# Attention and two feed-forward layers on one core: ScalarE's table load moved behind the last pair's copy, and a planner with other step times and due times

## The chip, the core and the metric

The program runs on one NeuronCore of a Trainium2 chip. TensorE (PE in the rows) multiplies, VectorE (DVE), ScalarE (ACT) and GpSimd (POOL) work on tiles, and SyncE (SP) issues the transfers. The metric is the device time of one execution in microseconds; lower is better.

## The reference

```python
# q, k, v: (4, 12, 448, 64); weights 768 x 2048 and 2048 x 768, twice
q_n, k_n = rmsnorm(q, g_q), rmsnorm(k, g_k)
scores = q_n @ k_n^T / sqrt(64); attn = softmax(scores)
x = (attn @ v) transposed to 1792 tokens x 768
h = x @ w_in;   x = (h * sigmoid(h)) @ w_out      # layer 1
h = x @ w2_in;  out = (max(h, 0) ** 2) @ w2_out   # layer 2
```

## The kernel before

**Stages.** Attention takes 24 pairs of heads one after the other, to about 271 us. Layer 1 takes the tokens in two halves (two batches of 448 tokens each) and the 2048 inner columns in four quarters, which makes eight segments, up to about 737 us. Layer 2 again takes two halves, and in each eight groups of 256 inner columns. Every product is made in higher precision from two parts of each operand: an upper part (a cast), a lower part (a subtraction), and three products. In most of layer 1 and all of layer 2 the products of 2 x 2 blocks are made by seven instead of eight block products (function `seven`, line 1104, nine matmuls of 448 columns each); only the first segment multiplies plainly (`up`, line 1017). The down products stand on line 1201 (layer 1, 448 columns), and on lines 1443 and 1568 (layer 2, 384 columns).

**Weights.** They arrive as 64-bit numbers. `words` loads a block into `raw` (two buffers, line 913, on SyncE's queue), and ScalarE makes the upper word (`magnitude`, line 920) and the lower bits (`low`, line 925); VectorE joins them (`merge`, line 932). `parts` splits the result into an upper and a lower part (lines 549 or 551, and 558).

**Order.** A hand-written table gives the times of all attention steps and fixes their order. All other steps are ordered by a planner (class `Plan`) when the program is built: it goes through the steps with a duration for each engine on which a step may run, and takes at each point the step that can start first, by its due time among equals. So it also chooses between VectorE, ScalarE and GpSimd for copies, casts and subtractions. Its inputs are the durations (`dve_t`, `pool_t`, `any_t`, `pe_t`, `SWITCH`, `PROD`) and `DUE`, a table that moves the due times of kinds of steps by stage. Each engine then runs its own list in that order, and waits where data or a buffer is missing.

**ScalarE's table.** `exp` in attention and `silu` in layer 1 need different tables of the engine. The program has no call for the load; it stands in ScalarE's list right ahead of the first activation that needs it: before, the first `silu`.

**The place after attention.** TensorE makes the first products of layer 1 into three PSUM banks of tag `t`, and a bank comes free when `silu` (line 1029) has read it. The last pair's result is copied out of PSUM by ScalarE (`pv_copy`, line 537).

Of the kernel before, what the change touches and what calls it, by code (L numbers as in the profile page):

```python
# [8 lines left out]
F32 = mybir.dt.float32  # L9
# [3 lines left out]
AF = mybir.ActivationFunctionType  # L13
# [3 lines left out]
P = 128  # L17
# [81 lines left out]
class Step:  # L99
# [10 lines left out]
LAG = {"pe": 0.21, "act": 0.13, "dve": 0.12, "pool": 0.12, "sp": 1.9, "none": 0.0}  # L110
SELF = {"pe": 0.0, "act": 0.1, "dve": 0.1, "pool": 0.06, "sp": 1.9, "none": 0.0}
FORM = {"scores": "rows", "attend": "columns"}
SWITCH = 0.16
ENGINES = ("pe", "act", "dve", "pool", "sp", "none")
ROUNDS = 8
AHEAD = 25.0
DUE = {
    "end0": {"acc": 4.25, "down2": -1, "h_hi": 21.25, "h_lo": 3.75, "keep_parts2": -1.25, "load_y": -0.75, "p1_copy": 3.75, "prod": 0.25, "square": 1, "u_sum": -0.5, "w_hi2": -6, "w_lo2": -0.75, "w_sum": -0.75, "y_hi": 5.25, "y_lo": 4.25, "y_sum": -3.5},
    "end1": {"acc": 2, "down2": -11.25, "h_hi": 16, "h_lo": 2.5, "h_sum": -39.5, "join": 18, "keep_parts2": -11.75, "load_parts2": -2.25, "load_word2": 1.75, "load_y": 0.5, "p1_copy": 0.5, "prod": 2, "square": 21.25, "store": -1.25, "u_sum": -1, "w_hi2": 4.25, "w_sum": -4.5, "y_lo": -3, "y_sum": 2.5},
    "now": {"ident": 5.75, "swap_pools": -0.5},  # L120
    "seg0": {"add": -0.5, "down": 3, "g_hi": 0.5, "g_lo": 0.75, "keep": 10.25, "load_raw": -6, "load_y": 0.5, "low": 1, "magnitude": -2, "merge": -6, "out1": -1, "p1_copy": 4, "part": 0.5, "prod": 4.75, "silu": 0.5, "store_y": -1, "u_sum": 2.75, "up": 2.5, "w_hi": 4.5, "w_lo": 6.25, "w_sum": -2, "y_hi": 0.75, "y_lo": 1, "y_sum": 2},
    "seg1": {"add": -4.25, "down": -4.5, "g_hi": 2.25, "g_lo": 5, "keep2": 45.25, "load_raw2": 6, "load_word": -5.5, "load_y": -0.75, "low2": -1.5, "magnitude2": -3, "merge2": -4.5, "p1_copy": -6.25, "part": -3.75, "prod": -3.25, "silu": -5.75, "store_y": 7, "u_sum": 2.25, "w_hi": 1.75, "w_lo": 1, "w_sum": -3, "y_hi": 10, "y_lo": 0.75, "y_sum": 2.5},
}


# [280 lines left out]
def kernel(  # L406
# [13 lines left out]
    nc = tc.nc  # L420
# [51 lines left out]
    def dve_t(n, rate=960.0, lock=False):  # L472
        return {"dve": (0.07 + n / rate, None, lock)}

    def pool_t(n, rate=474.0):
        return {"pool": (0.145 + n / rate, None, True)}

    def any_t(n, rate=474.0):
        return {**dve_t(n, 960.0, True), **pool_t(n, rate)}

    def copy_t(n):
# [2 lines left out]
    def pe_t(t):  # L484
        return {"pe": (t, None, False)}
# [13 lines left out]
    for n, src in enumerate((g_q, g_k)):  # L499
        for h in range(2):  # L500
# [4 lines left out]
                writes=[(graw, (n, h))],  # L505
# [46 lines left out]

        step(kind, when, copy_t(n), copy, reads=reads, writes=writes)

    def lower_part(kind, when, o, a, h, n, reads, writes, rate=474.0):

        step(
            kind, when, any_t(n, rate), lambda e: engine(e).tensor_tensor(o(), a(), h(), ALU.subtract),  # L558
            reads=reads, writes=writes,
        )  # L560

    def prepare(i):
# [88 lines left out]
        for n in range(2):  # L651
            n32 = sa([CP, NCH, 2, D], F32, "n")
            step(
                "norm", at, any_t(W2, 600.0),
                lambda e, n=n, n32=n32: engine(e).tensor_tensor(
                    n32.ap.rearrange("p c h d -> p h c d"),
                    qk.ap[:, n].rearrange("p (h c) d -> p h c d", h=2),
                    y.ap[:, n].rearrange("p (h c) -> p h c", h=2).unsqueeze(3).to_broadcast([CP, 2, NCH, D]),
                    ALU.mult),
                reads=[y, (qk, n)], writes=[n32],  # L660
            )
            plan.fix(i, "norm", j=n, at="dve" if i < 2 else "pool")
            pt = psum("t")

            def turn(e, n32=n32, pt=pt):
                for c in range(NCH):
                    nc.tensor.transpose(  # L667
                        pt.ap[:, c * CP:(c + 1) * CP], n32.ap[:, c].rearrange("p h d -> p (h d)"), ident.ap)

            step("turn_q", at, pe_t(0.384), turn, reads=[n32, ident], writes=[pt])  # L670
            plan.fix(i, "turn_q", j=n)

            def upper(e, n=n, pt=pt):
                o, a_ = T.ap[:, n, 0], pt.ap[:, :S]
# [32 lines left out]
    def weigh(i, T):  # L707

        PT = [sa([CP, NB8, CT, CP], F32, "PT") for _ in range(NCH // CT)]
        sums = sb([CP, 2, NCH], F32, "sum", 3)  # L710
        for c in range(NCH):
            at = ("pair", i, c)
            E = sa([CP, 2, S], F32, "E")
            pts = [psum("s"), psum("s")]

            def scores(e, c=c, pts=pts):
                for k_, (a, b_) in enumerate(((0, 0), (0, 1), (1, 0))):
                    for j in range(2):
                        r = slice(j * D, (j + 1) * D)
                        nc.tensor.matmul(  # L720
                            pts[j].ap[:CP, :S], T.ap[r, 0, a, c * CP:(c + 1) * CP], T.ap[r, 1, b_],
                            start=(k_ == 0), stop=(k_ == 2),
                        )

            step("scores", at, pe_t(0.606), scores, reads=[(T, (n, a)) for n in range(2) for a in range(2)], writes=pts)
            plan.fix(i, "scores", c)
            for j, pt in enumerate(pts):
                mx = sa([CP, 1], F32, "mx", 6)
                step(
                    "row_max", at, {"dve": (0.535, None, False)},  # L730
                    lambda e, pt=pt, mx=mx: nc.vector.tensor_reduce(  # L731
                        mx.ap, pt.ap[:CP, :S], AX.X, ALU.max, negate=True),
                    reads=[pt], writes=[mx],
                )
                plan.fix(i, "row_max", c, j)
                step(
                    "exp", at, {"act": (0.62, None, False)},
                    lambda e, j=j, c=c, pt=pt, mx=mx, E=E: nc.scalar.activation(  # L738
                        E.ap[:, j], pt.ap[:CP, :S], AF.Exp, bias=mx.ap, accum_out=sums.ap[:, j, c:c + 1]),
                    reads=[pt, mx], writes=[(E, j), (sums, (j, c))],  # L740
                )
                plan.fix(i, "exp", c, j)
                pe = psum("t")

                def turn(e, j=j, pe=pe, E=E):
                    for m in range(NCH):
                        nc.tensor.transpose(  # L747
                            pe.ap[:CP, m * CP:(m + 1) * CP], E.ap[:, j, m * CP:(m + 1) * CP], ident.ap)

                step("turn_e", at, pe_t(0.384), turn, reads=[(E, j), ident], writes=[pe])  # L750
                plan.fix(i, "turn_e", c, j)
                copy_step(
                    "e_copy", at, ECOPY[c][j], lambda c=c, j=j: PT[c // CT].ap[:, j * NCH:(j + 1) * NCH, c % CT, :],
                    lambda pe=pe: pe.ap[:CP, :S].rearrange("p (m t) -> p m t", t=CP), S, [pe], [(PT[c // CT], (c % CT, j))],
                )
                plan.fix(i, "e_copy", c, j)
        return PT, sums

    def attend(i, vr, PT, sums):
# [32 lines left out]
        for c2, pt in enumerate(PT):  # L792

            def products(e, c2=c2, pt=pt):
# [9 lines left out]
                        )  # L804

            step(
                "attend", at, pe_t(1.456), products,
                reads=[vr] + [(pt, (c, j)) for c in range(CT) for j in range(2)], writes=[(pv, c2)],
            )
            plan.fix(i, "attend", c2)  # L810
# [4 lines left out]
            "pv_copy", at, ("act", "dve"), lambda: t.ap, lambda: pv.ap[:, :S], S,  # L815
            [(pv, c2) for c2 in range(len(PT))], [t])
        plan.fix(i, "pv_copy", at="act")
        step(
            "attended", at, any_t(S),
            lambda e: engine(e).tensor_tensor(t.ap, t.ap, R.ap, ALU.mult),  # L820
# [216 lines left out]
    FD = 2  # L1037
    halves = {}
    W3 = HC * P
    PROD = 9 * 0.2065  # L1040

    def view(b, a, c):

# [641 lines left out]
```

## Time and profile before

| | us |
|---|---|
| median of 3 runs | 1165.32 |
| lowest and highest | 1164.49, 1168.14 |
| the profiled execution | 1167.08 |
| its span, first to last instruction | 1165.3 |
| TensorE busy in it | 1147.8 |
| VectorE, ScalarE, GpSimd busy | 939.3, 632.3, 287.9 |

In the rows a line such as `PE t L1104` names the engine, the tile that is written and the line of the program. A duration of a matmul holds its pipeline, so consecutive ones overlap; how fast they follow each other is read from their starts. The granted clock (PEclk) is the share of 2.4 GHz that TensorE was given: 1.00 is 2.4 GHz, 0.50 is 1.2 GHz.

### The profile page before, as it was taken

The numbers are of one execution on the slowest core, as the hardware profiler recorded it, in microseconds if no ns is written. First come the engines' busy times: TensorE is split into PE (matmuls) and PEld (weight loads), VectorE is DVE, ScalarE is ACT, GpSimd is POOL, SyncE is SP. The second block draws the span as 40 slices with busy tenths as digits, with TensorE's granted clock in tenths as the row PEclk, the third lists the DMA queues.
The fourth block names the chain that finished last, engine by engine and source line by source line (L and its number), as shares of the span: only waits on it lengthen the run. The fifth ranks groups of instructions, "written<-read, shape, count | busy, mean of one in ns | idle before, by whom it ended". The sixth has DMA issues, their size and how long they took to land.

```text
span 1165.3 us, 19244 instructions
## 1 busy us (share of the span) xinstructions
PE 1147.8 (99%) x6817; PEld 1018.8 (87%) x6817; DVE 939.3 (81%) x1685; ACT 632.3 (54%) x1290; POOL 287.9 (25%) x507
## 2 busy tenths in 40 slices
PE   7999999998999999999999999999999999999998
PEld 5777777777999999999999999999998999999997
DVE  7888888886876868996878698588888976888876
ACT  5999999985554444555535353543433535333321
POOL 4566676632000101210111021001121120122220
PEclk8999999999999999999999999999999999999999
DMA  6566768578855564778776849977777696555444
GB/s 175 94 103 115 105 109 111 99 125 175 275 167 185 172 212 133 263 236 273 244 238 209 272 145 329 337 271 261 286 264 260 217 378 230 177 176 190 164 163 135
DMA packets 142064, 235.22 MB, mean 202 GB/s; under 512 B 32016, under 2 KB 105744, under 8 KB 141968
## 3 DMA queue, kind: packets, MB, share of 16 engines
q1 hardware_dynamic: 141728, 233.80, 67.2%
q8 instruction: 54, 0.88, 0.3%
q14 instruction: 42, 0.34, 0.1%
q10 hardware_dynamic: 240, 0.20, 0.1%
HBM read 157.58 MB, written 76.37 MB: 201 GB/s over the span
## 4 chain that ended last, share of the span: by engine, by line
PE 91%; DVE 4%; ACT 2%; DMA 1%; issue 1%; SPq 0%; POOL 0%; ACTq 0%; DVEq 0%; POOLq 0%
PE t L1104 22%; PE s L1201 20%; PE s L1443 11%; PE pv L1104 9%; PE t L747 7%; PE pv L797 7%; PE s L720 6%; PE s L1568 6%; PE t L1017 2%; PE t L667 2%; DMA raw<-in_moe_w_out_dram 1%; DVE gg L1462 1%; DVE w L558 1%; DVE g L1119 0%; DVE g L1500 0%
## 5 line engine op out<-in xcount | busy, mean ns | idle before, releaser
L1201 PE MATMUL s<-gg,w 128*128 128x448 f32 x1152 | 240.4, 367 | 0.0
L1201 PEld LDWEIGHTS s<-gg,w 128*128 128x128 f32 x1152 | 216.2, 188 | 19.8 <-DVE g L1213 0.3
L1119 DVE TENSOR_TENSOR g<-t,g 128x448 f32<-128x448 f32 x180 | 108.8, 619 | 63.9 <-PE t L1104 53.1
L1443 PE MATMUL s<-w,gh 128*128 128x384 f32 (+1 forms) x564 | 143.0, 334 | 2.1 <-DVE gg L1462 1.1
L738 ACT ACTIVATE E<-s,mx 112x448 f32<-112x448 f32 x192 | 122.9, 653 | 13.7 <-ACT xf L537 7.9
L731 DVE TENSOR_REDUCE mx<-s 112x1 f32<-112x448 f32 x192 | 107.4, 611 | 14.4 <-PE s L720 14.1
L1462 DVE TENSOR_TENSOR gg<-s,gg 128x384 f32<-128x384 f32 (+1 forms) x197 | 102.6, 547 | 18.1 <-PE s L1443 17.7
L558 DVE TENSOR_TENSOR w<-W,w 128x768 fp32r<-128x768 f32 (+1 forms) x123 | 111.7, 917 | 4.2 <-ACT w L549 3.3
L1443 PEld LDWEIGHTS s<-w,gh 128*128 128x128 f32 x564 | 101.8, 188 | 4.0 <-DVE gg L1462 1.9
L1104 PE MATMUL t<-yb,w 128*128 128x448 f32 x468 | 103.1, 367 | 0.2 <-DVE w L558 0.2
L747 PEld LDWEIGHTS t<-ident,E 112*112 112x112 f32 x768 | 73.8, 134 | 32.5 <-issue 19.1
L549 ACT CAST w<-W 128x768 fp32r<-128x768 f32 (+1 forms) x74 | 54.9, 744 | 83.8 <-PE s L1201 31.9
L747 PE MATMUL t<-ident,E 112*112 112x112 f32 x768 | 94.7, 266 | 1.2 <-ACT E L738 1.2
L1368 ACT ACTIVATE g<-g 128x448 f32<-128x448 f32 x48 | 27.7, 578 | 124.6 <-DVE g L1119 124.1
L1443 PE MATMUL s<-w,gl 128*128 128x384 f32 (+1 forms) x282 | 94.3, 335 | 0.3 <-POOL gl L558 0.3
L1104 PEld LDWEIGHTS t<-yb,w 128*128 128x128 f32 x468 | 87.6, 188 | 8.1 <-DVE w L558 0.5
L797 PE MATMUL pv<-PT,vv 112*64 112x224 f32 x768 | 83.0, 359 | 0.1
L720 PE MATMUL s<-T 64*112 64x448 f32 x576 | 73.8, 388 | 1.3 <-ACT T L676 1.2
L1104 PE MATMUL pv<-xb,w 128*128 128x448 f32 x324 | 72.4, 367 | 0.0
L539 DVE COPY PT<-t 112x448 f32<-112x448 f32 x96 | 59.1, 618 | 11.6 <-PE t L747 11.5
L797 PEld LDWEIGHTS pv<-PT,vv 112*64 112x64 f32 x768 | 51.0, 136 | 20.0 <-ACT xf L537 0.3
L1104 PEld LDWEIGHTS pv<-xb,w 128*128 128x128 f32 x324 | 60.7, 188 | 5.5
(168 smaller groups left out, 2213.1 us busy)
## 6 DMA issues: line engine op xcount, KB each, us to landing
raw<-in_moe_w_in_dram SPq DMA_DIRECT2D x32, 768.0 KB
raw<-in_moe_w_out_dram SPq DMA_DIRECT2D x24, 512.0 KB
raw<-in_moe_w_out_dram SPq DMA_DIRECT2D x16, 768.0 KB
su<-w SPq DMA_DIRECT2D x16, 768.0 KB
w<-su SPq DMA_DIRECT2D x16, 768.0 KB
xf<-y SPq DMA_DIRECT2D x48, 224.0 KB
xf<-x SPq DMA_DIRECT2D x39, 224.0 KB
ki<-W SPq DMA_DIRECT2D x16, 384.0 KB
```

The source lines that it names most:

```text
L558: kind, when, any_t(n, rate), lambda e: engine(e).tensor_tensor(o(), a(), h(), ALU.subtract),
L720: nc.tensor.matmul(pts[j].ap[:CP, :S], T.ap[r, 0, a, c * CP:(c + 1) * CP], T.ap[r, 1, b_], start=(k_ == 0), stop=(k_ == 2),)
L731: lambda e, pt=pt, mx=mx: nc.vector.tensor_reduce(mx.ap, pt.ap[:CP, :S], AX.X, ALU.max, negate=True),
L738: lambda e, j=j, c=c, pt=pt, mx=mx, E=E: nc.scalar.activation(E.ap[:, j], pt.ap[:CP, :S], AF.Exp, bias=mx.ap, accum_out=sums.ap[:, j, c:c ...
L747: nc.tensor.transpose(pe.ap[:CP, m * CP:(m + 1) * CP], E.ap[:, j, m * CP:(m + 1) * CP], ident.ap)
L797: nc.tensor.matmul(pv.ap[j * D:(j + 1) * D, c2 * CT * CP:(c2 + 1) * CT * CP], vr.ap[:, j * NCH + m, :], pt.ap[:, j * NCH + m].rearrange("p ...
L1104: nc.tensor.matmul(pt.ap[:, :S], w_()[:, c0 + c, :], view(b, a, c)(), start=(start and c == 0 and k == 0), stop=(c == HC - 1 and k == 2), ...
L1119: lambda e: nc.vector.tensor_tensor(o.ap, pt.ap[:, :S], a.ap, ALU.add),
L1201: nc.tensor.matmul(pt.ap[:, :S], w_()[:, f, :], gg.ap[:, k, a, f, :], start=(f == 0 and n == 0), stop=(f == HQ - 1 and n == 2),)
L1443: nc.tensor.matmul(pt.ap[:, :en], g.ap[:, fi, c0:c0 + P], w_()[:, 0, e0:e0 + en], start=(n == 0), stop=(n == 5),)
L1462: "acc", at, dve_t(n), lambda e: nc.vector.tensor_tensor(o(), pt.ap[:, :n], o(), ALU.add),
L1568: nc.tensor.matmul(pt.ap[:, :NH], a[i][0](m), b[j][0](), start=(start and k == 0), stop=(k == 2), skip_group_check=True,)
```

## The change

Three things change. First, a new step `table` behind the last pair's `pv_copy`: a `silu` of one column, whose result nobody reads, so that the table load stands there. Second, durations in the planner: GpSimd's subtraction of 448 columns goes from 1.09 to 1.18 us, transposes from 0.384 to 0.406, `attend` from 1.456 to 1.512, `PROD` from 1.8585 to 1.8252, `SWITCH` from 0.16 to 0.13. Third, other numbers in `DUE`. The arithmetic that the output is made of stays the same.

```diff
-SWITCH = 0.16
+SWITCH = 0.13
...
 DUE = {
...
-    "now": {"ident": 5.75, "swap_pools": -0.5},
+    "now": {"ident": 12.75},
...
-    def pool_t(n, rate=474.0):
-        return {"pool": (0.145 + n / rate, None, True)}
+    def pool_t(n, rate=415.0):
+        return {"pool": (0.1 + n / rate, None, True)}
...
-            step("turn_q", at, pe_t(0.384), turn, reads=[n32, ident], writes=[pt])
+            step("turn_q", at, pe_t(0.406), turn, reads=[n32, ident], writes=[pt])
...
-                "attend", at, pe_t(1.456), products,
+                "attend", at, pe_t(1.512), products,
...
         plan.fix(i, "pv_copy", at="act")
+        if i == len(pairs) - 1:
+            first = sb([P, 1], F32, "first", 1)
+            step(
+                "table", ("seg", 0, 0.0), {"act": (1.4, None, False)},
+                lambda e: nc.scalar.activation(first.ap, t.ap[:, :1], AF.Silu), reads=[t], writes=[first],
+            )
...
-    PROD = 9 * 0.2065
+    PROD = 9 * 0.2028
```

The new lines move later line numbers by 6 (line 1029 becomes 1035). The order of every engine is the same up to the end of attention, except for three places of `magnitude` and `low` in ScalarE's list. What follows are places where it differs.

ScalarE's list from the last pair's copy (`xf<-pv`) on; `W<-raw` and `raw<-raw` are `magnitude` and `low`, `g<-t` is `silu`. Before:

```order
L537 COPY xf<-pv 128x448
L920 ACTIVATE W<-raw 128x512
L925 ACTIVATE raw<-raw 128x512
L1029 ACT_TABLE_LOAD
L1029 ACTIVATE g<-t 128x448
L549 CAST gg<-g 128x448
```

And with the change:

```order
L537 COPY xf<-pv 128x448
L822 ACT_TABLE_LOAD
L822 ACTIVATE first<-xf 128x1
L549 CAST w<-W 128x768
L926 ACTIVATE W<-raw 128x512
L931 ACTIVATE raw<-raw 128x512
L1035 ACTIVATE g<-t 128x448 x2
L549 CAST gg<-g 128x448
```

The load moved ahead of `magnitude`, a cast of 768 columns came from VectorE's list, and the first two `silu` stand together.

VectorE's list at the third to last group of layer 2's first half, up to the accumulation (`gg<-s,gg`) for which TensorE waits at 881.01 us of the trace; `g<-t,g` adds products, `W<-W` are `w_sum`, `gl`, `v` and `w` from two operands are lower parts. Before:

```order
L1119 TENSOR_TENSOR g<-t,g 128x448 x2
L1462 TENSOR_TENSOR gg<-s,gg 128x384
L1119 TENSOR_TENSOR g<-t,g 128x448
L1062 TENSOR_TENSOR W<-W 128x384
L551 CAST v<-W 128x384
L1062 TENSOR_TENSOR W<-W 128x384
L558 TENSOR_TENSOR gl<-g,gh 128x448
L1081 TENSOR_TENSOR W<-W 128x384
L1462 TENSOR_TENSOR gg<-s,gg 128x384
```

And with the change:

```order
L1125 TENSOR_TENSOR g<-t,g 128x448
L558 TENSOR_TENSOR gl<-g,gh 128x448
L1125 TENSOR_TENSOR g<-t,g 128x448 x2
L1068 TENSOR_TENSOR W<-W 128x384 x2
L558 TENSOR_TENSOR v<-W,v 128x384
L1087 TENSOR_TENSOR W<-W 128x384
L551 CAST gh<-g 128x448
L1468 TENSOR_TENSOR gg<-s,gg 128x384
```

Two lower parts `gl` and the lower part of `v` came from GpSimd, the cast of `v` went to ScalarE, and an accumulation went ahead of the piece. Further ahead a square of `g` and a cast of 768 columns went to ScalarE.

TensorE's list at the end of layer 2's first half, ahead of the first down product of the last group (`s<-w,gh`, with `s<-w,gl` behind it). Before:

```order
L1104 MATMUL pv<-xb,w 128x448 x9
L1104 MATMUL t<-xc,w 128x448 x9
L1104 MATMUL t<-part,w 128x448 x9
L1443 MATMUL s<-w,gh 128x384 x2
L1443 MATMUL s<-w,gl 128x384
```

And with the change:

```order
L1110 MATMUL t<-xc,w 128x448 x9
L1110 MATMUL t<-part,w 128x448 x9
L1110 MATMUL pv<-raw,w 128x448 x9
L1449 MATMUL s<-w,gh 128x384 x2
L1449 MATMUL s<-w,gl 128x384
```

A product of the second half, nine matmuls, came ahead of the down product. Over the whole program GpSimd's list has 19 instructions less, VectorE's 6 more and ScalarE's 14 more.

## Rows read from the trace of the kernel before

**Rows 1.** The page's first part: busy time, share of the span, instructions.

```profile
PE 1147.8 (99%) x6817; PEld 1018.8 (87%) x6817; DVE 939.3 (81%) x1685; ACT 632.3 (54%) x1290; POOL 287.9 (25%) x507
```

**Rows 2.** TensorE's waits after 300 us: total us, times, longest.

```profile
PE s L1568 <- DVE part L558: 1.1, 2, 0.8
PE s L1443 <- DVE gg L1462: 1.1, 1, 1.1
PE s L1443 <- DVE gh L551: 0.8, 1, 0.8
PE s L1443 <- POOL gl L558: 0.3, 1, 0.3
PE t L1104 <- DVE w L558: 0.2, 1, 0.2
```

**Rows 3.** The chain that ended last, at the first `w_out` block: start, us.

```profile
269.79 10.34 DMA raw<-in_moe_w_out_dram
```

**Rows 4.** Timeline of ScalarE: start, us, instruction [idle before <- releaser].

```profile
271.70 0.53 ACT L537 COPY xf<-pv 128x448 f32<-128x448 f32 x1 [1.30 <-PE pv L797]
280.20 0.66 ACT L920 ACTIVATE W<-raw 128x512 f32<-128x512 f32 x1 [7.97 <-DMA raw<-in_moe_w_out_dram]
...
281.42 1.28 ACT L1029 ACT_TABLE_LOAD   x1
282.71 0.54 ACT L1029 ACTIVATE g<-t 128x448 f32<-128x448 f32 x1
```

**Rows 5.** Timeline of TensorE behind its wait in the first segment.

```profile
283.31 2.58 PE L1017 MATMUL t<-xc,w 128*128 128x448 f32 x9 [3.00 <-ACT g L1029]
285.69 6.83 PE L1017 MATMUL t<-xb,w 128*128 128x448 f32 x27
292.36 0.99 PE L1017 MATMUL t<-xc,w 128*128 128x448 f32 x4
```

**Rows 6.** Stretches: length, busy us (instructions) by engine, PEclk, DMA share, GB/s.

```profile
284.00:288.00 4.00, 4.00 (x14) 3.55 (x14) 4.00 (x7) 2.19 (x4) 1.22 (x1) 0.59 1.06 335
288.00:292.00 4.00, 4.00 (x21) 3.65 (x20) 3.20 (x7) 2.24 (x4) 1.56 (x1) 0.99 0.54 191
300.00:511.00 211.00, 211.00 (x1022) 191.63 (x1021) 173.05 (x297) 103.97 (x174) 19.04 (x13) 1.00 0.63 201
515.00:735.00 220.00, 220.00 (x1087) 203.59 (x1086) 170.73 (x284) 107.37 (x170) 30.74 (x22) 1.00 0.75 250
```

**Rows 7.** Timeline of TensorE where the second token half begins.

```profile
511.85 2.10 PE L1104 MATMUL t<-xc,w 128*128 128x448 f32 x9
513.79 2.03 PE L1104 MATMUL t<-xb,w 128*128 128x448 f32 x9
515.65 1.98 PE L1104 MATMUL t<-yb,w 128*128 128x448 f32 x9
517.47 0.57 PE L1104 MATMUL pv<-gh,w 128*128 128x448 f32 x2
```

**Rows 8.** Timeline of all engines at the accumulation wait in layer 2.

```profile
878.24 1.83 POOL L558 TENSOR_TENSOR w<-W,w 128x768 fp32r<-128x768 f32 x1 [0.35 <-ACT w L549]
878.29 2.20 DVE L1081 TENSOR_TENSOR W<-W 128x384 f32<-128x384 f32 x1
...
880.88 0.54 DVE L1081 TENSOR_TENSOR W<-W 128x384 f32<-128x384 f32 x1
...
881.01 0.61 PE L1443 MATMUL s<-w,gh 128*128 128x384 f32 x2 [1.13 <-DVE gg L1462]
...
881.34 0.61 DVE L558 TENSOR_TENSOR gl<-g,gh 128x448 fp32r<-128x448 f32 x1
```

**Rows 9.** Stretches, columns as in rows 6: end of the first half; layer 2.

```profile
450.00:512.00 62.00, 62.00 (x301) 56.10 (x301) 56.53 (x100) 32.02 (x56) 12.22 (x8) 1.00 0.61 204
737.00:1166.00 429.00, 420.65 (x2222) 397.17 (x2220) 343.05 (x615) 163.29 (x298) 74.85 (x62) 1.00 0.64 230
```

**Rows 10.** Timeline of TensorE at a wait for weights in layer 2.

```profile
773.05 1.89 PE L1104 MATMUL t<-yb,w 128*128 128x448 f32 x8 [0.19 <-DVE w L558]
```

More of the change, by code (lines that the diff above doesn't have):

```diff
@@ L117 @@
 DUE = {
-    "end0": {"acc": 4.25, "down2": -1, "h_hi": 21.25, "h_lo": 3.75, "keep_parts2": -1.25, "load_y": -0.75, "p1_copy": 3.75, "prod": 0.25, "square": 1, "u_sum": -0.5, "w_hi2": -6, "w_lo2": -0.75, "w_sum": -0.75, "y_hi": 5.25, "y_lo": 4.25, "y_sum": -3.5},
-    "end1": {"acc": 2, "down2": -11.25, "h_hi": 16, "h_lo": 2.5, "h_sum": -39.5, "join": 18, "keep_parts2": -11.75, "load_parts2": -2.25, "load_word2": 1.75, "load_y": 0.5, "p1_copy": 0.5, "prod": 2, "square": 21.25, "store": -1.25, "u_sum": -1, "w_hi2": 4.25, "w_sum": -4.5, "y_lo": -3, "y_sum": 2.5},
@@ L120 @@
-    "now": {"ident": 5.75, "swap_pools": -0.5},
-    "seg0": {"add": -0.5, "down": 3, "g_hi": 0.5, "g_lo": 0.75, "keep": 10.25, "load_raw": -6, "load_y": 0.5, "low": 1, "magnitude": -2, "merge": -6, "out1": -1, "p1_copy": 4, "part": 0.5, "prod": 4.75, "silu": 0.5, "store_y": -1, "u_sum": 2.75, "up": 2.5, "w_hi": 4.5, "w_lo": 6.25, "w_sum": -2, "y_hi": 0.75, "y_lo": 1, "y_sum": 2},
-    "seg1": {"add": -4.25, "down": -4.5, "g_hi": 2.25, "g_lo": 5, "keep2": 45.25, "load_raw2": 6, "load_word": -5.5, "load_y": -0.75, "low2": -1.5, "magnitude2": -3, "merge2": -4.5, "p1_copy": -6.25, "part": -3.75, "prod": -3.25, "silu": -5.75, "store_y": 7, "u_sum": 2.25, "w_hi": 1.75, "w_lo": 1, "w_sum": -3, "y_hi": 10, "y_lo": 0.75, "y_sum": 2.5},
+    "end0": {"down2": -1.5, "h_hi": 50.5, "h_lo": -0.75, "keep_parts2": 4.25, "load_y": -0.25, "prod": -0.75, "relu": 2.25, "square": -8.25, "u_sum": 5.25, "w_hi2": 0.25, "w_lo2": 1.25, "w_sum": -3.75, "y_hi": 1.5, "y_lo": -0.75, "y_sum": -2.75},
@@ new lines @@
+    "end1": {"acc": 2, "h_hi": 39.25, "h_lo": 7.5, "h_sum": -6.25, "join": 5.5, "load_parts2": 0.5, "load_word2": -6.5, "load_y": 0.5, "p1_copy": -0.25, "prod": 47.25, "relu": -2.5, "square": 0.5, "store": -2.75, "u_sum": 7.25, "w_hi2": -1, "w_lo2": -0.25, "w_sum": -4.5, "y_hi": 0.5, "y_lo": 13.5, "y_sum": 0.25},
+    "now": {"ident": 12.75},
+    "seg0": {"add": -5, "down": -0.5, "g_hi": -0.75, "g_lo": 2, "load_raw": -0.5, "load_y": 4.5, "low": 3.75, "magnitude": -0.75, "merge": -2, "out1": 2.5, "p1_copy": 2.75, "part": -0.25, "prod": -0.25, "silu": -8.5, "store_y": 4, "u_sum": -3.25, "up": -1.75, "w_hi": -0.25, "w_lo": 0.25, "w_sum": -0.75, "y_hi": 1.75, "y_lo": -6},
@@ L123 @@
+    "seg1": {"add": -11.25, "down": -1.75, "g_hi": 1, "g_lo": 6.25, "keep2": 58.5, "load_raw2": 3, "low2": 21, "magnitude2": 8, "merge2": -5.75, "out1": -42.25, "p1_copy": -1.5, "part": 1, "silu": -1.5, "store_y": -15, "u_sum": 0.25, "w_hi": 4.75, "w_lo": 1, "y_hi": 5.75},
 }
@@ L473, in dve_t, with any_t @@
         return {"dve": (0.07 + n / rate, None, lock)}
-    def pool_t(n, rate=474.0):
-        return {"pool": (0.145 + n / rate, None, True)}
-    def any_t(n, rate=474.0):
+    def pool_t(n, rate=415.0):
+        return {"pool": (0.1 + n / rate, None, True)}
+    def any_t(n, rate=415.0):
         return {**dve_t(n, 960.0, True), **pool_t(n, rate)}
@@ L553, in upper_part, with lower_part @@
         step(kind, when, copy_t(n), copy, reads=reads, writes=writes)
-    def lower_part(kind, when, o, a, h, n, reads, writes, rate=474.0):
+    def lower_part(kind, when, o, a, h, n, reads, writes, rate=415.0):
         step(
@@ L748, in turn @@
                             pe.ap[:CP, m * CP:(m + 1) * CP], E.ap[:, j, m * CP:(m + 1) * CP], ident.ap)
-                step("turn_e", at, pe_t(0.384), turn, reads=[(E, j), ident], writes=[pe])
+                step("turn_e", at, pe_t(0.406), turn, reads=[(E, j), ident], writes=[pe])
                 plan.fix(i, "turn_e", c, j)
```

## The prediction

> **What bounds the kernel now.** I read the page's busy shares first [rows 1]: TensorE is busy 1147.8 us of a 1165.3 us span, VectorE 81%, ScalarE 54%. So the end is set by TensorE, and a change of order can win in two ways only: fewer idle gaps on TensorE, or matmuls that follow each other faster. Next the waits of TensorE after the first 300 us [rows 2]: five small ones, 3.5 us in sum, all in layer 2. Ahead of them, behind the start phase that this change leaves alone, stands one large one: 3.00 us before the matmul at 283.31, on the activation of line 1029 [rows 5].
>
> That wait is read from the DMA queue, ScalarE and TensorE side by side. The load of the first block of `w_out` goes out at 269.79 and takes 10.34 us [rows 3]. ScalarE copies the last pair's `pv` at 271.70, then stands for 7.97 us behind that block; at 280.20 it runs `magnitude` and `low` on it, at 281.42 it loads its table for 1.28 us, and only at 282.71 comes the first `silu`, which frees the PSUM bank that TensorE needs [rows 4]. TensorE ran out at 280.3 and goes on at 283.31 [rows 5].
>
> The wait costs more than itself. In 284 to 288 us the granted clock is 0.59 on average and 14 matmuls run where the next 4 us hold 21 [rows 6]: a stretch at the 1.2 GHz level, after an engine that had stood for 3.0 us. The 36 matmuls from 283.31 to 292.36 take 9.05 us [rows 5]; at 0.2065 each (below) they would take 7.43. That is 1.6 us, of which 0.1 is the restart itself: 1.5 us for the clock.
>
> The last view is the pace of TensorE while it never waits. Lines 1104 and 1201 run the same shapes in both token halves, yet 300 to 511 us hold 1022 matmuls in 211 us (0.2065 each) and 515 to 735 us hold 1087 in 220 us (0.2024 each), both at a granted clock of 1.00 [rows 6]. The timeline shows where it turns, and that a short hold stands there: from 511.85 nine matmuls take 1.94 us to the next group's start, the next nine 1.86, and from 515.65 on nine take 1.82 [rows 7], which is 0.2022 each. So a stream of 448-column matmuls has two paces, 2% apart, and it changed from the slow one to the fast one at a pause. The stream that follows the half-clock stretch is in the slow one.
>
> **The change part by part.** *The one-column activation.* The order of ScalarE shows the table load directly behind the `pv` copy, in the 7.97 us in which ScalarE waits for data [rows 4]. It adds 1.28 us of load, one activation of one column (under the 0.54 of 448 columns) and, moved here from VectorE, one cast of 768 columns (at most 0.93, an estimate from the 0.54 by columns): 2.75 us under a cover of 7.97. Without that cover the 1.28 would stay and the cast would come on top. Behind the block's landing nothing changes but the load: the first `silu` starts 1.28 us earlier. Term: 1.28 us.
>
> The Trainium skill says otherwise about the price: "ScalarE: Activation LUTs", section "What ACT_TABLE_LOAD costs", puts a switch at about 1.28 us of load and another 1.38 us of drain. The trace agrees with the load, and shows no drain: the `silu` starts 0.01 us after it [rows 4]. By the page the gain here would be 2.66 us, an estimate that would bring the time 1.4 us lower.
>
> *What is late next.* TensorE goes on at 282.03: its gap is 1.7 us where it was 3.0. That leaves the question of the clock. After a gap of 1.1 us in layer 2 [rows 8] the granted clock stays at 1.00, through all of layer 2 [rows 9]; after one of 3.0 it falls [rows 6]. The gain is 1.5 us by the one row and nothing by the other. I take it that the clock stays at 2.4 GHz, since the 1.1 us gap is nearer (0.6 away against 1.3).
>
> *The pace.* If the clock stays, the stream restarts from a pause at the full clock, as it did at 511.85, and nothing in layer 1 stops it again: the list of waits holds none in it before 511 us [rows 2]. The stretch from 288.2 to 511.8 is 223.6 us, 1083 matmuls at 0.2065; at 0.2024 it is 4.4 us shorter [rows 6]. Bounds: nothing (the pace stays slow, or the clock falls as before) and 4.7 us (0.2022 each, by the nine from 515.65 [rows 7]). I take 4.4. It hangs on the same condition as the clock.
>
> *Step times and due times.* They change the order of all engines from the end of attention on. TensorE's order moves by single steps; GpSimd loses 19 instructions, VectorE gets 6 more, ScalarE 14. In layer 1 there is nothing to win, since TensorE waits nowhere else; after the pace changes the others have 2% less time, and VectorE is busy 56.5 of 62 us in the last part of the first half [rows 9], which leaves room. In layer 2 I see three waits that the new order touches. (a) At 881.01 TensorE waits 1.13 us for an accumulation that stands behind a `w_sum` of 2.20 us; its sister takes 0.54, and GpSimd was in a subtraction of 1.83 us beside it [rows 8]. That these go together is my reading of one case. In the new order that `w_sum` has one GpSimd subtraction less beside it, and the square and one cast ahead of it are gone to ScalarE; against that VectorE gets three subtractions. Between 0 and 1.5; I take 1.2. (b) At 773.05 a product waits 0.2 us for its weights' lower part [rows 10]; a down product of six matmuls, about 1.0 us, now stands ahead of it. 0.2. (c) The one wait on `gl` [rows 2], 0.3 us, is that of a group's first down product; nine matmuls now stand ahead of it (the last piece of order in the section on the change), 1.8 us by their 0.2022 to 0.2065. 0.3. The sum is 1.7. The new order will make waits of its own: the old one has 3.5 us of them in layer 2 [rows 2], and its successor is not free of what makes them. I charge 0.7, a fifth of that, with bounds of 0 and 3.5. Net gain 1.0, between a loss of 1.8 and a gain of 1.7.
>
> *The sum.* 1.28 + 1.5 + 4.4 + 1.0 = 8.2 us. The profiled execution took 1167.08 us, 1.8 around its span, and would come to 1158.9. The median of the runs is 1165.32, so the profiled one is 1.8 slower than the median; from the median the same gain gives 1157.1 us.
>
> **The rivals.** *First, the clock falls all the same.* A gap of 1.7 us stands between the two rows that I have, and the landing of the block moves from run to run with the DMA queue. If the block lands 0.5 to 1 us later, the gap comes near the old one. Then 1.5 and 4.4 are not won: 1165.3 - 1.28 - 1.0 = 1163.0 us. For it speaks that nothing in the change makes that block land earlier.
>
> *Second, no gap at all.* If the block lands 1.9 us earlier than in this profile, TensorE does not stop. It wins the gap and the clock (3.0 + 1.5 + 1.0 = 5.5), but the stream also keeps the slow pace: 1159.8, and if the short hold at 511.85 goes too, the fast pace of the second half is lost as well, 4.4 us: 1164.2. Against it: the load took 10.34 us [rows 3], and its place in the queue is the old one.
>
> *Third, slower.* In layer 2 TensorE waits for VectorE's accumulations already [rows 2], and VectorE is busy 343 of 429 us there [rows 9]. The order moves a net 9 steps of layer 2 onto it, at 0.61 us each, a subtraction of 448 columns [rows 8]: 5.5 us. If nothing hides them and the clock falls as in the first rival, the time is 1165.3 - 1.3 + 5.5 = 1169.5. It decides once VectorE's queue is the late one at each accumulation, that is when waits in layer 2 grow from 3.5 to over 8 us [rows 2]. Against it: GpSimd loses 13 steps there, and each of those that ran beside VectorE could hold it by 1 us or more, as at 878.29 [rows 8].
>
> **How the numbers follow.** The measurement tells changes of over 0.3% (3.5 us) from none: under 1161.8 is faster, over 1168.8 slower. Forecast 0.48 at 1157.1 (1154.5 to 1160 by its bounds), first rival 0.34 at 1163.0 (1161 to 1164.5), second 0.09, third 0.09. Faster: the forecast, half of the second and a sixth of the first: 0.48 + 0.05 + 0.06 = 0.59. Slower: most of the third, 0.08. The rest, 0.33, is within. The range from 1154.5 to 1164.5 leaves out the third rival and the tails.
>
> **What would show it.** Step one is right if ScalarE's table load follows the `pv` copy and the first `silu` starts right behind `low`, and TensorE's wait on the first part of layer 1 is 1.5 to 2.0 us. Step two if the granted clock is 1.00 from 25 us on. Step three if 300 to 511 us hold about 1042 matmuls and not 1022, and nine matmuls take 1.82 us on both sides of 500 us. Step four if layer 2 shows under 3 us of waits and the one behind the 2.20 us `w_sum` is gone. I am wrong if the clock falls after the shorter gap, if the stream at full clock restarts in the slow pace, or if layer 2 waits for VectorE in places where the old order did not.

## The result, and the profile after

The changed kernel takes 1172.29 us in the median of 8 runs (1170.74 to 1175.87), the kernel before 1165.22 (1159.56 to 1168.14): a ratio of 1.0051, 95% interval 1.003 to 1.0073. It is slower, by half a per cent; the forecast was 1157.1, in a range of 1154.5 to 1164.5.

The page's first part, and below it TensorE's waits from 272 us on (total us, times, longest):

```profile
PE 1146.6 (98%) x6817; PEld 1019.9 (87%) x6817; DVE 946.6 (81%) x1691; ACT 639.5 (55%) x1304; POOL 263.4 (23%) x488
```

```profile
PE s L1574 <- DVE part L558: 5.5, 7, 1.5
PE s L1207 <- DVE g L1219: 1.1, 2, 0.8
PE s L1574 <- ACT gg L1465: 1.1, 1, 1.1
PE s L1449 <- ACT gh L549: 1.0, 1, 1.0
PE s L1207 <- DVE w L558: 0.9, 1, 0.9
PE t L1023 <- ACT g L1035: 0.8, 1, 0.8
PE s L1574 <- ACT part L549: 0.8, 1, 0.8
PE s L1449 <- DVE gh L551: 0.5, 1, 0.5
PE s L1207 <- DVE gg L558: 0.5, 1, 0.5
```

The place after attention went as forecast. ScalarE's timeline there:

```profile
270.06 0.54 ACT L537 COPY xf<-pv 128x448 f32<-128x448 f32 x1 [0.43 <-PE pv L797]
270.61 1.28 ACT L822 ACT_TABLE_LOAD   x1
271.90 0.20 ACT L822 ACTIVATE first<-xf 128x1 f32<-128x1 f32 x1
...
278.44 0.66 ACT L926 ACTIVATE W<-raw 128x512 f32<-128x512 f32 x1 [5.60 <-issue]
279.00 0.64 ACT L931 ACTIVATE raw<-raw 128x512 int32<-128x512 uint16 x1
279.54 0.96 ACT L1035 ACTIVATE g<-t 128x448 f32<-128x448 f32 x2
```

The load lies in the time in which ScalarE waits for data, and the first `silu` follows `low` at once. TensorE's wait, 3.00 us before [rows 5], is 0.8 in the list above. From `magnitude` on the block to TensorE's next matmul it is 1.68 us (278.44 to 280.12, the start of the next fence), where it was 3.11 [rows 4, rows 5]: 1.4 us less, for a forecast of 1.28. The rest of what the stop lost is the block, which came earlier: ScalarE began on it 8.50 us after layer 1's first matmul, where it was 9.45. The next fence is TensorE's timeline from there, and the last one the stretches (columns as in rows 6):

```profile
280.12 2.09 PE L1023 MATMUL t<-xc,w 128*128 128x448 f32 x9 [0.81 <-ACT g L1035]
282.05 5.63 PE L1023 MATMUL t<-xb,w 128*128 128x448 f32 x27
287.52 1.99 PE L1023 MATMUL t<-xc,w 128*128 128x448 f32 x9
...
300.29 23.71 PE L1207 MATMUL s<-gg,w 128*128 128x448 f32 x114
323.84 0.36 PE L1110 MATMUL pv<-xb,w 128*128 128x448 f32 x1
```

```profile
284.00:288.00 4.00, 4.00 (x22) 3.70 (x21) 3.51 (x6) 2.28 (x5) 1.28 (x1) 1.00 1.06 303
300.00:511.00 211.00, 209.90 (x1022) 191.21 (x1020) 175.30 (x291) 108.63 (x181) 26.69 (x17) 1.00 0.64 208
515.00:735.00 220.00, 218.63 (x1062) 199.09 (x1061) 172.45 (x283) 106.50 (x168) 16.02 (x11) 1.00 0.74 246
```

Three things are to be seen. The granted clock stays at 1.00 behind the shorter stop. The stream runs at the fast pace at once, (287.52 - 282.05) / 27 = 0.2026 us each, but only as far as the first long stream of `gg`: there it is (323.84 - 300.29) / 114 = 0.2066. And the second token half, where nothing was to change, holds 1062 matmuls in the 220 us that held 1087 [rows 6].

Where the time went, by these rows: the profiled spans are 1168.8 and 1165.3, 3.5 apart. TensorE starts layer 1 0.8 us earlier (269.94 against 270.75), its stop is 2.2 shorter and the clock saves 1.5, 4.5 us in all. From 300 to 511 us the counts are equal, 1022: what the pace wins on some products is lost to waits. From 515 to 735 us 25 matmuls are missing, 5.1 us at 0.2024. The rest, 3.5 + 4.5 - 5.1 = 2.9 us, is lost in layer 2, net. TensorE's waits behind 300 us are 11.4 us in sum where they were 3.5 [rows 2].

### The profile page after: what moved, and what is told of

Same layout as the page of the kernel before. It is cut to its first block, busy times and chain, and to the rows that moved or that the text cites. A ratio compares the mean times of both kernels' runs of the same rounds, so it can differ in the third digit from the quotient of the medians.

```text
span 1168.8 us, 19246 instructions
## 1 busy us (share of the span) xinstructions
PE 1146.6 (98%) x6817; PEld 1019.9 (87%) x6817; DVE 946.6 (81%) x1691; ACT 639.5 (55%) x1304; POOL 263.4 (23%) x488
## 4 chain that ended last, share of the span: by engine, by line
PE 88%; DVE 8%; issue 1%; ACT 1%; DMA 1%; SPq 0%; DVEq 0%
PE t L1110 21%; PE s L1207 18%; PE s L1449 12%; PE pv L1110 8%; PE t L747 7%; PE pv L797 7%; PE s L720 6%; PE s L1574 6%; PE t L1023 2%; PE t L667 2%; DVE g L1125 1%; DVE gg L1468 1%; DVE part L558 1%; DMA w<-sz 1%; DVE w L558 1%
## 5 line engine op out<-in xcount | busy, mean ns | idle before, releaser
L1207 PE MATMUL s<-gg,w 128*128 128x448 f32 x1152 | 243.2, 369 | 2.5 <-DVE g L1219 1.1
L549 ACT CAST w<-W 128x768 fp32r<-128x768 f32 (+1 forms) x87 | 65.0, 749 | 83.8 <-PE s L1207 32.9
```

Source lines behind the costliest of these rows:

```text
L1207: nc.tensor.matmul(pt.ap[:, :S], w_()[:, f, :], gg.ap[:, k, a, f, :], start=(f == 0 and n == 0), stop=(f == HQ - 1 and n == 2),)
```

## The experiments

All kernels run beside the kernel before on the same chip. Its median there was 1168.6 to 1169.8 us, so only ratios to it are compared between batches. In the single traces the end of attention varies by some 9 us (layer 1 starts between 269.94 and 279.32 us); what is read from traces is read behind it.

**The question of the pace.** The new tile `first` has 4 bytes in each partition and takes 32. It is allocated between the weights' tile `w` and `g`, so in the built program every later tile (`gg`, `yb`, `gh`, `gl`, `part`, `v`) starts 32 bytes further on; `xb`, `xc`, `raw` and `w` stay. By *distance* I mean the start of the moving tile less that of `w`, modulo 256: it is 0 for all of them before, and in the changed kernel 32 for the tiles that were moved.

*Padding alone, 32 bytes (before_pad).*

```diff
+        if tag == "g" and not pad:
+            pad.append(cp.tile([P, 1], F32, tag="pad", name="pad", bufs=1))
```

> The kernel before with one edit: an unused tile of 4 bytes is allocated where the changed kernel allocates `first`, so g, gg, yb, gh, gl, part and v start 32 bytes later. No instruction is added or moved. Address theory: the second token half loses its fast pace on gg, yb, gh and gl, about 800 matmuls of 4.0 ns, 3.2 us: 515 to 735 us hold about 1071 matmuls where the kernel before holds 1087, with gg steady at 206.7 ns; xb and xc may be at 202.6 in both halves, which gives back up to 1.5 us in the first. In all 1165 to 1169 us. Order theory: nothing changes, 1165.2 us and 1087 matmuls.

Measured: 1169.28 us, ratio 1.0009 (0.999 to 1.0028). The time fits both theories; the pace decides. The second token half shows it, where the kernel before has its fast pace. TensorE's timeline at a long stream of `gg` there, in the kernel before and in before_pad:

```profile
529.63 24.48 PE L1201 MATMUL s<-gg,w 128*128 128x448 f32 x120
553.95 0.57 PE L1104 MATMUL pv<-gh,w 128*128 128x448 f32 x2
```

```profile
530.51 24.95 PE L1208 MATMUL s<-gg,w 128*128 128x448 f32 x120
555.30 0.58 PE L1111 MATMUL pv<-gh,w 128*128 128x448 f32 x2
```

24.32 / 120 = 0.2027 has become 24.79 / 120 = 0.2066, as in the changed kernel, without one instruction more or less, and 515 to 735 us hold 1070 matmuls where the kernel before holds 1087 [rows 6]. So the pace on `gg` is made by the address and not by the order. In time it costs little against the kernel before, since that runs its first half at 0.2065 anyway [rows 6].

*The changed kernel with 64 bytes (after_64), and with all tiles 32 bytes further as well (after_all0).*

```diff
-            first = sb([P, 1], F32, "first", 1)
+            first = sb([P, 16], F32, "first", 1)
```

after_all0 has this line and widens `graw`, ahead of all large tiles, by 32 bytes.

> The changed kernel with one edit: the new one-column tile `first` is 64 bytes wide instead of 4, so every tile allocated behind it (g, gg, yb, gh, gl, part, v) starts 64 bytes later than in the kernel before and not 32. The order of all engines is that of the changed kernel. Address theory (a 448-column matmul whose moving tile starts on a multiple of 64 bytes follows its predecessor at 206.7 ns, on 32 beyond one it can follow at 202.6): the 1962 matmuls with gg, yb, gh, gl and part as moving tile lose 4.0 ns each, 7.8 us, so about 1164.5 us; 515 to 735 us hold 1080 matmuls or more where the changed kernel holds 1062; layer 2 keeps its new waits. Order theory (the new order and its waits cost the time, the address plays no part): 1172 us, 1062 matmuls, as the changed kernel.

> The changed kernel with two tiles widened (`graw` by 32 bytes, `first` to 64), so that all moving tiles and all weight tiles start on multiples of 64 bytes; order unchanged. If the moving tile's own start decides: xb, xc and raw become slow too, 1224 matmuls of 4.0 ns, 4.9 us over the changed kernel, 1177 us. If it is a mismatch between the moving tile (0) and the weights (32) that is slow: everything is fast, 1164.5 us. Order theory: 1172 us.

Measured: 1167.76 us, ratio 1.0004 (0.9983 to 1.0025), and 1167.49, ratio 0.9982 (0.9964 to 1.0001). The stream of `gg` in after_64, and in after_all0:

```profile
308.43 22.96 PE L1207 MATMUL s<-gg,w 128*128 128x448 f32 x114
331.23 1.99 PE L1110 MATMUL pv<-xb,w 128*128 128x448 f32 x9
```

```profile
309.26 22.97 PE L1207 MATMUL s<-gg,w 128*128 128x448 f32 x114
332.07 1.99 PE L1110 MATMUL pv<-xb,w 128*128 128x448 f32 x9
```

0.2000 and 0.2001: faster than either pace of the kernel before. From 515 to 735 us both hold 1084 matmuls where the changed kernel holds 1062. Against the changed kernel's ratio of 1.0051 after_64 wins some 5.5 us (3.5 of uncertainty); 7.8 were expected. In after_all0 `gg` and `w` start 32 bytes further on than in after_64, both of them, and the pace is the same. So my first form of the address theory (a multiple of 64 bytes is slow) is wrong. What counts is the distance between the two tiles that TensorE reads: in before_table96 (below) `gg` stands 96 bytes further on than in the kernel before, just as in after_all0 (32 and 64), only `w` differs, and the pace there is 0.2053.

*Padding alone, 64 bytes (before_64).* The edit of before_pad with 16 columns instead of 1.

> The kernel before with one edit: an unused tile of 64 bytes where the changed kernel allocates `first`, so gg, yb, gh, gl and part start 64 bytes beyond the weights' tile w, modulo 128. No instruction is added or moved. Distance theory: the 1962 matmuls with these as moving tile run at 200 ns; against a mix of 206.7 (first half, layer 2) and 202.7 (second half) in the kernel before that is 6.7 ns for about 1150 and 2.7 ns for about 800, 9.9 us at most, and 5 us if the kernel before is often in the 202.7 pace: 1160 to 1165 us where the kernel before takes 1169.8. If the gain of before_table came from the table load alone: no change.

Measured: 1161.01 us, ratio 0.9932 (0.9907 to 0.9958): some 8 us from 64 unused bytes. The stream of `gg`:

```profile
310.85 25.37 PE L1208 MATMUL s<-gg,w 128*128 128x448 f32 x126
336.06 1.99 PE L1111 MATMUL pv<-xb,w 128*128 128x448 f32 x9
```

*The table step alone, at 64, 128 and 96 bytes (before_table, before_table128, before_table96).* The order before; the activation is issued with the last `pv` copy:

```diff
+            nc.scalar.copy(t.ap, pv.ap[:, :S])
+            if last:
+                first = cp.tile([P, 16], F32, tag="first", name="first", bufs=1)
+                nc.scalar.activation(first[:, :1], t.ap[:, :1], AF.Silu)
```

with 32 or 24 columns in the other two.

> The kernel before, its order and its addresses, with the one-column silu alone added directly behind the last pair's copy (its tile 64 bytes wide), so that the table load stands there. No other instruction moves. By steps one to three of the prediction: 1.3 + 1.5 + 4.4 = 7.2 us less, 1158 us; TensorE's wait in the first segment is 1.7 us, the granted clock stays 1.00 behind it, 300 to 511 us hold about 1040 matmuls. If the pace does not come with the clock: 1162.4 us and 1022 matmuls. If the clock falls all the same: 1163.9 us.

> The kernel before with the one-column silu behind the last pair's copy, as in the run before_table, but its tile is 128 bytes wide: each moving tile keeps the distance to the weights' tile w that it has in the kernel before, modulo 128 (0 for gg, yb, xb, xc). This is the prediction's steps one to three with nothing else changed. Pace as a state (the prediction): the stream restarts from a gap of about 1.6 us at full clock and stays at 202.7 ns, 300 to 511 us hold 1040 matmuls, 7.2 us less than before. Distance theory (distance 0 can run in either pace, 64 bytes runs at 199.9): the same 202.7 or 206.7, slower than the run before_table by 1962 matmuls of 2.8 ns, 5.5 us, or more.

> As before_table, but the added tile is 96 bytes wide: gg, yb, gh, gl and part start 96 bytes beyond w, modulo 128. Distance theory: if the pattern repeats every 128 bytes, 96 is as 32 bytes short of the weights, at which the products of xb by v ran 204 to 205 ns in the changed kernel; gg then runs at 204 to 205, 8 to 10 us slower than the run before_table. If a pace as a state is all there is: 202.7 or 206.7 for all products alike.

Measured: 1160.11 us, ratio 0.993 (0.9907 to 0.9953); 1166.73, ratio 0.9983 (0.9963 to 1.0003); 1166.65, ratio 0.9982 (0.9961 to 1.0002). The stream of `gg` in before_table128, and in before_table96:

```profile
312.44 25.86 PE L1206 MATMUL s<-gg,w 128*128 128x448 f32 x126
338.14 1.99 PE L1109 MATMUL pv<-xb,w 128*128 128x448 f32 x9
```

```profile
315.45 26.03 PE L1206 MATMUL s<-gg,w 128*128 128x448 f32 x126
341.32 1.98 PE L1109 MATMUL pv<-xb,w 128*128 128x448 f32 x9
```

0.2040 and 0.2053. The pace at 96 is about where the distance theory put it, 0.204 to 0.205. Against before_table, though, 0.9982 / 0.993 = 1.0052 is 6 us, less than the 8 to 10 expected. 128, which I had taken to be like 0, has a pace of its own. So before_table128, meant as the trial of the prediction's first three steps with nothing else changed, changed the pace too; it won 2.0 us (between 4.3 won and 0.4 lost) and not 7.2. before_table at 64 won 8, but for another reason: before_64, without the step, won as much. In time the step is 0.9930 against 0.9932, with some 4 us of uncertainty, so a gain of 1 or 2 us can't be seen in it.

The trace of before_table shows the single step as it was meant: the stop is 1.25 us and the clock stays at 1.00 behind it.

```profile
289.36 2.10 PE L1022 MATMUL t<-xc,w 128*128 128x448 f32 x9 [1.25 <-ACT g L1034]
```

But the stop depends on when the `w_out` block lands. In the thirteen other traces that have this order of the place it is 0.8, 1.6, 1.8, 2.0, 2.7, 2.8, 2.8, 2.9, 3.1, 3.5 and 4.7 us with the step, and 3.8 and 4.9 without (3.00 in the kernel before [rows 5]). The step's own share does not vary: from `magnitude` on the block to TensorE's next matmul it is 1.68 or 1.69 us in all twelve traces with the step ahead of the block, and 3.10 or 3.11 in the three without it, the kernel before among them. What varies is when ScalarE can begin on the block, between 8.50 and 12.52 us after layer 1's first matmul, nearly three times what the step saves. In these traces the granted clock stayed at 1.00 behind the stops up to 1.6 us and fell behind those from 1.8 on.

*The changed order at 128 bytes (after_128).* The line of after_64 with 32 columns.

> The changed kernel with the added tile 128 bytes wide instead of 4: the order is that of the changed kernel, the distances of tiles are those of the kernel before, modulo 128. Address theory: gg, yb, gh, gl and part no longer run at 206.7 for certain; at 202.7 it is 1962 times 4.0 ns, 8 us, faster than the changed kernel, and the new order's own price against the run before_table128 is the 7 to 8 us that after_64 stands behind before_table. If the 206.7 of the changed kernel came from its order: no gain.

Measured: 1175.16 us, ratio 1.0058 (1.0035 to 1.0081); `gg` runs at 0.2039. Against before_table128 that is 1.0058 / 0.9983 = 1.0075, and at 64 bytes after_64 against before_table is 1.0004 / 0.993 = 1.0075 too: the order costs 8.7 us (some 4 of uncertainty) at either distance.

*All products at 64 (all_64), and a better order of the place after attention (best).* all_64 is before_table with 192 bytes of padding ahead of `w`: with `first`'s 64 that is 256 bytes, so `xb`, `xc`, `gg` and `yb` are all at distance 64. best adds:

```diff
+        late = {n for n in order if steps[n].when == ("seg", 0, 0.5)
+                and steps[n].kind in ("magnitude", "low", "merge", "w_hi", "w_lo")}
...
+        order = rest[:k + 1] + [n for n in order if n in late] + rest[k + 1:]
```

> As before_table (order before, table step, 64 bytes at the added tile), with 192 bytes of padding ahead of w as well: xb, xc, raw, gg and yb all start 64 bytes beyond w modulo 128, gg and attention's tiles lie as before modulo 256, and xb stands at distance 0 to v. Distance theory: the xb and xc products by w, 950 or so at 202.7 to 206 in before_table, come down to 200: 2.5 to 4 us faster than before_table. If only the place of gg and yb matters: as before_table.

> As all_64, and the five steps on the first w_out block (magnitude, low, merge, w_hi, w_lo) stand behind the second silu of layer 1 in the order of ScalarE and VectorE, not ahead of the first. If TensorE's stop after attention is ScalarE standing behind that block: the stop is gone whenever the block lands, the granted clock stays at 1.00, and the time is 3 to 4.5 us under all_64's share of the kernel before (about 0.9895 of it, 1157.5 us). If the block is needed there anyway (for the first down product): the stop comes back later in the first segment and nothing is won.

Measured: 1160.77 us, ratio 0.9927 (0.99 to 0.9954), and 1159.5, ratio 0.9917 (0.9893 to 0.9941). In all_64 the first products, on `xc` and `xb`, run at 0.2000 as well, (305.16 - 299.76) / 27:

```profile
299.76 1.96 PE L1029 MATMUL t<-xc,w 128*128 128x448 f32 x9
301.56 3.76 PE L1029 MATMUL t<-xb,w 128*128 128x448 f32 x18
305.16 1.96 PE L1029 MATMUL t<-xc,w 128*128 128x448 f32 x9
```

The gain over before_table that I expected does not show in the ratios, which cannot tell 2.5 us apart; all_64's own trace has a stop of 3.1 us and the half clock behind it. In best the stop after attention is gone, but the second of the two cases came true: TensorE stops some 10 us later (296.76 against the 286.67 of the old place), behind the third `silu`, which stands behind a cast of the same block. The granted clock stayed at 1.00 there, so the length of a stop alone does not decide that.

```profile
288.47 5.57 PE L1036 MATMUL t<-xb,w 128*128 128x448 f32 x27
296.76 2.08 PE L1036 MATMUL t<-xc,w 128*128 128x448 f32 x9 [2.72 <-ACT g L1048]
```

It is still the fastest kernel of the study in ratio, though not apart from before_64, before_table and all_64. All four beat both kernels.

**The question of the order.** *One layer at a time (new_seg, new_end).* Order and engines of one layer's steps are taken from the changed kernel, the other layer's from the kernel before; table step and 64 bytes as in before_table.

```diff
+        for k, m in enumerate(other):
+            start[m] = int.from_bytes(bytes(raw[j * n + k] for j in range(4)), "little") / 1000
...
```

> As before_table (table step, 64 bytes, order before), but all steps of layer 1 stand in the changed kernel's order and on its engines; layer 2 keeps the order before. After_64 and before_table differ by 4.0 us between matmuls 2550 and 4650 of their traces (layer 1) and by 2.7 between 4650 and the end. If the new order's price lies where these traces show it: 4 us slower than before_table, with holds of TensorE near 482, 487, 689 and 700 us. If it comes from what crosses the border of the layers: no slower, or by all 7.6 us.

> The other half: layer 2 in the changed kernel's order, layer 1 in the order before, table step and 64 bytes as in before_table. By the same traces: 2.7 us slower than before_table, no holds in layer 1 but one near 706 us, and five to seven waits of 0.8 us or more for `part` in the second half of layer 2; the wait near 877 us is gone.

Measured: 1165.05 us, ratio 0.9966 (0.994 to 0.9992), and 1176.7, ratio 1.0066 (1.0042 to 1.009). new_seg is 0.9966 / 0.993 = 1.0036 of before_table, 4.2 us, near the 4 expected; and after_64, which has layer 2 new as well, is 1.0004 / 0.9966 = 1.0038 of new_seg, another 4.4, each with some 4 of uncertainty. In new_seg's trace the holds near 482 and 487 us are there again and the one near 689 is not, and 1.5 us at 739.63, a wait for weights where the two orders were joined, belongs to neither order. So that both layers have a share is likely and not shown by the times alone; the traces of before_table and after_64 say the same, 4.0 us in layer 1 (from matmul 2550 to 4650) and 2.7 behind it. new_end is a bad test. Its largest wait is one that neither order has, 6.2 us for a weights' part that comes late where the two orders were joined:

```profile
PE pv L1165 <- DVE w L614: 6.7, 2, 6.2
PE s L1629 <- DVE part L614: 4.6, 6, 1.5
```

*What makes VectorE late (gl_dve, l1_dve).* In after_64's trace one subtraction for `part` takes 1.47 to 1.50 us in each of the last six groups of layer 2, and in five of them TensorE waits for `part`. GpSimd, VectorE and TensorE in one of them:

```profile
1068.61 1.15 POOL L558 TENSOR_TENSOR gl<-g,gh 128x448 fp32r<-128x448 f32 x1 [1.70 <-ACT gh L549]
1068.68 1.95 DVE L558 TENSOR_TENSOR part<-g,part 128x384 fp32r<-128x384 f32 x2
...
1070.22 1.48 PE L1574 MATMUL s<-xb,part 128*128 128x384 f32 x7 [0.69 <-DVE part L558]
```

Two subtractions of 0.55 us each take 1.95, beside one of GpSimd's of 1.15. gl_dve gives that one to VectorE, in six groups, and l1_dve six others in layer 1:

```diff
+        for m in range(4298, 4819, 104):
+            assert self.steps[m].kind in ('h_lo',) and at[m] == "pool"
+            at[m] = "dve"
```

> The run after_64 (changed order, 64 bytes) with six instructions moved: in the last six groups of layer 2 one lower part of 448 columns (`gl` from `g` and `gh`) is made by VectorE, behind its two subtractions for `part`, where GpSimd made it beside them. In after_64's trace one of those subtractions takes 1.47 to 1.50 us each time, beside a GpSimd subtraction of 1.13 to 1.49 us, where its sister takes 0.55, and TensorE waits 0.4 to 1.5 us for `part`, 4.6 us in six waits. If VectorE is late there because GpSimd holds it: the subtractions take 0.55, the waits for `part` fall to under 1.5 us in sum, and the kernel is 3 to 4 us faster than after_64 (0.997 of the kernel before). If VectorE's own queue is late: 0.61 us more on it in each group, the waits stay or grow, 1.000 to 1.002.

> The run after_64 with six other GpSimd subtractions made by VectorE at their place in the order, those that run right ahead of TensorE's four holds in the second part of each token half of layer 1 (476.7, 480.6, 485.4, 684.1, 687.1 and 699.1 us of after_64's trace, 1.3 to 3.9 us each there). If VectorE is late at the holds because GpSimd holds it: the waits near 482, 487, 689 and 700 us, 3.5 us in sum, fall to under 1.5, 2 us faster than after_64. If it is VectorE's own queue: 0.61 to 0.68 us more in front of each, the waits stay or grow.

Measured: 1165.08 us, ratio 0.9962 (0.9937 to 0.9987), and 1164.85, ratio 0.9966 (0.994 to 0.9993), where after_64 had 1.0004. The same group in gl_dve, and its sum of waits for `part`, which was 4.6:

```profile
1067.65 1.01 DVE L561 TENSOR_TENSOR part<-g,part 128x384 fp32r<-128x384 f32 x2
1067.99 3.45 PE L1577 MATMUL s<-xb,part 128*128 128x384 f32 x18
1069.52 0.61 DVE L561 TENSOR_TENSOR gl<-g,gh 128x448 fp32r<-128x448 f32 x1
```

```profile
PE s L1577 <- DVE part L561: 0.9, 2, 0.6
```

VectorE has one instruction more in each group and is done with `part` sooner, after 1.01 us instead of 1.95. In layer 1 the same: the waits that were to go are 3.0 us in sum in after_64 and 1.0 in l1_dve. After_64's holds at 483 and 488 us, and l1_dve's one that is left there:

```profile
483.22 3.88 PE L1207 MATMUL s<-gg,w 128*128 128x448 f32 x18 [0.47 <-DVE g L1219]
487.99 0.47 PE L1207 MATMUL s<-gg,w 128*128 128x448 f32 x1 [0.89 <-DVE g L1219]
```

```profile
485.21 5.07 PE L1210 MATMUL s<-gg,w 128*128 128x448 f32 x24 [0.27 <-DVE g L1222]
```

For these twelve steps the cause is that GpSimd holds VectorE, and not VectorE's own queue. The traces give 2.8 us (between matmul 5850 and the end) and 2.5 (from 3300 to 4500; l1_dve's trace then waits 0.8 at 923.57 us for a transfer of weights, which after_64's does not) for the twelve steps, the ratios 4.9 and 4.4 with some 4 us of uncertainty each; that is 5 to 9 of the 8.7 us. What else is in the new order was not taken apart.

## Why the prediction was wrong

**Where TensorE waits, and the table load: right.** The load went into ScalarE's wait, the drain that the Trainium skill gives ("ScalarE: Activation LUTs", section "What ACT_TABLE_LOAD costs") does not show here either: the activation behind the load starts at 271.90, 0.01 us after it, and the path from the block to TensorE's next matmul got shorter by 1.4 us in every trace, where the term was 1.28. What I left out is that the stop as a whole hangs on the landing: I took the one landing time of the trace as given, and it moves by more than the load lasts.

**The clock: right in the changed kernel's trace, not in most.** I set the forecast at 0.48 and the first rival, the clock that falls all the same, at 0.34; of the twelve traces with the table step ahead of the first block three kept the clock and nine did not. The rival's reason, a landing that varies, was the right one: ScalarE began on the block 8.50 us after layer 1's first matmul in the changed kernel's trace and up to 12.52 in the others. That the changed kernel's trace kept the clock was luck.

**The pace: the step that failed first.** The rows were read rightly: two paces, 2% apart, and a fast one behind a pause. The account of it, a state of the stream that a pause sets and that nothing in layer 1 ends, was made from one change at 511.85 us and is wrong. The stream left the fast pace at 300.29 us without a pause, at the first product whose moving tile had been shifted. The 4.4 us did not come, and the second half lost 3.7 of what it had: 5.1 less the 1.4 us for which TensorE is not busy there (220.00 - 218.63). Of a new tile of 4 bytes the prediction counted the activation that writes it and the load ahead of it, and not its address.

**Step times and due times: wrong in sign and size.** I took a net gain of 1.0 us, by three waits that go and a flat 0.7 for what the new order would make; it costs 8.7 (some 4 of uncertainty). The three did go: no wait for an accumulation of the first half, for `gl` or for weights on the seven-product line is left in the list. The flat charge failed: waits grew by 7.9 us in the trace, 4.4 of them for `part` (5.5 where 1.1 was), in a loop that repeats one mishap in each of the last six groups. The third rival had the mechanism, VectorE late at what layer 2 waits for, and put it at 1169.5. But I argued against it that GpSimd has fewer steps, and that each could hold VectorE by 1 us; what decides is beside what the remaining ones stand: in the changed kernel GpSimd makes `gl` right beside `part`, for which TensorE waits. And "in layer 1 there is nothing to win" was taken to mean that nothing could be lost: it is about 4 us (4.2 by the ratios, 4.0 in the traces).

**The sum.** By the ratios of the runs: table step about 0, 32 bytes of distance +0.1%, the order +0.75%, together +0.8%, 10 us with some 5 of uncertainty, where the ratio of +0.51% is 6 us and the medians are 7.1 apart. The bounds beside the forecast don't come out of its terms: with the clock kept these add up to a gain between 1.0 and 9.2 us, 1164.3 to 1156.1, and not to 1154.5 to 1160. The measured time is outside both, mainly because the order's bound, a loss of 1.8 at most, was far too narrow.

What stays open: why the distance of two tiles sets the pace; why distance 0 has two paces in the kernel before, and what moves it from one to the other (the pause at 511.85 may or may not); what of the new order beyond the twelve steps costs time; and why attention ends up to 9 us later in some traces.

## What to carry to other kernels

A new buffer, however small, shifts all that are allocated behind it: where TensorE is the bound, compare the pace of equal matmuls by tile before and after, and try a few paddings, since that can be worth more than the change itself. When a planner reorders work, do not charge the new waits as a fraction of the old ones; look in the printed order for GpSimd's two-input work ahead of and beside VectorE's late results that read two tiles in SBUF, above all inside a loop. A stop that ends with a transfer's landing has a spread, and a gain smaller than that spread is not seen in a median.

## What the runs showed of the hardware

The pace of back-to-back 448-column matmuls at a granted clock of 1.00, by the distance of moving tile and weights: 0.2000 at 64 bytes, 0.2053 at 96, 0.2040 at 128, 0.2066 at 32, and 0.2024 or 0.2065 at 0. It was the same when both tiles were shifted together. The Trainium skill ("TensorE: Matmul & The Clock Gate", section "Back-to-back issue gap") gives, for a single matmul by itself and not for a stream, the columns by 2.4 GHz plus 2.5 ns, by estimate 0.1892 us here. No run here has a matmul by itself; the streams ran at 0.2000 to 0.2066, and for them the rows decide.

A two-input instruction of VectorE that was held beside one of GpSimd took 0.9 to 2.3 us where it takes 0.55 to 0.62 alone (384 or 448 columns). Yet of 209 two-input instructions that overlapped one of GpSimd's after 300 us in the changed kernel's trace only 21 were held, by 0.25 us or more. Which ones, the trace shows: 142 of the 209 read a tile in PSUM, and none of these was held; the 21 are among the 44 that read only SBUF and began inside a GpSimd instruction, and of the 23 that read only SBUF and began ahead of one none was held. Why the rest of the 44 got off with 0.2 us or nothing was not taken apart. The Trainium skill ("SBUF — State Buffer", section "SBUF: two separate sides") speaks of a pair of ports for which GpSimd contends with a VectorE instruction that has two inputs in SBUF: whichever starts first holds it for its whole instruction, and the other waits. The row at 1068.68 us of after_64's trace agrees, 1.95 for two of 0.55 beside 1.15, and so does that no instruction with an input in PSUM was held; by that rule more of the 44 should have been.
